# Which queue fetches the list of one pair: SyncE in one transfer in place of GpSimd in two

## The chip, the cores and the metric

The kernel runs on one core of a Trainium2 chip. The metric is device time in microseconds for one launch; less is better. Several executions of a kernel are taken, and their median is the figure that is compared. One further execution is recorded by the hardware profiler, and its trace is what the rest of this text reads.

## What is computed

A gated linear attention runs over 4 batches of 8 heads, 768 positions and 48 channels. Its output, 3072 tokens of 384 numbers, goes through a noisy top-2 router with 8 experts, each a two-layer network (384 to 1024 to 384).

```python
for t in range(S):                                   # attention
    state = alpha[:, :, t, :, None] * state + einsum('bhd,bhe->bhde', k[:, :, t], v[:, :, t])
    y[:, :, t] = einsum('bhd,bhde->bhe', q[:, :, t], state)
x = y.transpose(0, 2, 1, 3).reshape(B * S, H * D)
noisy = x @ w_gate + log1p(exp(x @ w_noise)) * noise  # router
top2 = argpartition(-noisy, 2, axis=1)[:, :2]         # with a softmax over the two as weights
for e in range(E):                                   # experts
    for k in range(2):
        mask = top2[:, k] == e
        out[mask] += top2_w[mask, k, None] * (maximum(x[mask] @ w1[e], 0) @ w2[e])
```

All numbers are float32.

## The kernel before

**Two stages that overlap.** In the first quarter of the span the attention is worked off in 24 chunks of 128 tokens. Each chunk's result is written to the DRAM tensor `x_rows`. The router runs along with it, in units of six chunks. For every token and each of its two experts it writes one entry of four numbers (token, weight, the other expert, rank) into the DRAM tensor `table`, at a row that belongs to the expert. That is done by 48 indirect transfers on GpSimd (`put_entries`, line 161), each of 128 entries of 16 bytes.

**Pairs.** The experts then take their tokens in 24 pairs of tiles, 256 list entries each. A list `order_of` (line 987) says which expert a pair belongs to: pairs 0 to 7 are the first 256 entries of experts 0 to 7, pairs 8 and 9 are two further parts of expert 7, pairs 10 and 11 of expert 6, and so on down to expert 0. A pair loads new weights only where its expert differs from that of the pair before (`is_new`, line 990), so pairs 8 and 9 use the weights that pair 7 loaded, and pair 10 is the next to load. After pair 7 there are three smaller "half" tiles in between, which start later than everything discussed here. The rows of the first 14 pairs (`PLANNED`, line 989) are known when the program is built; later ones are read from a computed plan.

**Steps of a pair.** `pair_steps(i)` (line 1184) gives each step of pair i a due time in units in which a pair takes T = 20. All steps of all pairs are sorted by due time and issued in that order; the tile framework does not reorder them (`tc.manual_schedule()`). So the due times set the order on each engine. [...] The steps that matter here, each with the due time relative to the pair's start:

- `load_tab` (-32, line 1016): fetches the pair's 256 entries from `table` into an on-chip tile `tab`. It may read any row, so it must wait for the table writes: pairs 0 to 7 for the writes of the first two of four router units, later pairs for all 48 (`take_tile`, line 169).
- `load_w1` (-29.5) and `load_w2` (-19.8): 1.5 MB of weights each, on SyncE. Each has two buffers, so a load waits until the expert two before it no longer needs the buffer.
- `find_rows` (-27; for pair 8 due at -21.5): six small VectorE operations on `tab` (lines 1046 to 1058) that give `where`, the row numbers for the gathers.
- `gather` (-26; for pair 8 -21): two indirect GpSimd transfers of 128 rows of `x_rows` into `x_in` (line 886).
- `turn_x` (-10.1, line 1064): TensorE transposes of `x_in` (line 1068).
- `product1`, `product2` (0 to 18.6, lines 1126 and 1133): TensorE products of the two layers, with VectorE sums in between (`plus`, `less`, lines 1073 to 1077). Twice per pair TensorE adds to a bank that VectorE must first have read.
- `get_prev` (8.5, line 871), `combine` (20.9, line 1158), `put_pair` (22.2, line 879): rows of `out` that already hold the token's first expert are fetched, added to and written back, by indirect transfers on GpSimd. A fetch waits for all earlier writes of `out`.

With these due times `load_tab(8)` is due at 128. On GpSimd it stands behind the last two table writes (due 125 and 126.3) and ahead of `get_prev(6)` (128.5) and `gather(8)` (139). `find_rows(8)` (138.5) stands in VectorE's queue in the midst of pair 6's last sums and pair 7's first.

**Queues.** `load_tab` puts its transfers on SyncE (SP) or on GpSimd (POOL), by pair. SP's queue otherwise holds only the weight loads in this stage. Every transfer takes one of eight completion semaphores per kind of queue in rotation, and a transfer also waits for the one eight places earlier.

Of the kernel before, what the change touches and what calls it, by code (L numbers as in the profile page):

```python
# [18 lines left out]
def kernel(  # L19
# [32 lines left out]
    nc = tc.nc  # L52
    B, H, S, D = q.shape
    N, DM = out.shape
    E, _, F = moe_w1.shape
# [113 lines left out]
    def take_tile(get, units=NU):  # L169
        count = 1 + 2 * UT // C * units  # L170
        for put in entries[:count]:
            tc.add_manual_dep(get.ins, put.name, AFTER, reason="reads any row of the table that these fill")
        for put in entries[count:]:
            tc.declare_no_dep(get.ins, put, reason="rows behind those of the tile")
        taken.append(get.ins)
# [714 lines left out]
    def of_plan(i, what, most, engine=mybir.EngineType.SP):  # L890
        return nc.values_load(plan[0:1, i, what:what + 1], engines=[engine], min_val=0, max_val=most,
                              skip_runtime_bounds_check_because=WHY)
# [101 lines left out]
    def pairs(on):  # L994
# [20 lines left out]

        def load_tab(i):

            by, engine = (nc.sync, mybir.EngineType.SP) if i < 2 or 5 <= i < E else (nc.gpsimd, mybir.EngineType.Pool)
            row = order_of[i] * RMAX + [0, R2, 2 * R2][rounds[i]] if i < PLANNED else of_plan(FIRST_PAIR + i - E, 1, TROWS - R2, engine)
            tabs[i] = on["tab"].tile([C, 2, 8], F32, name="tab")  # L1020
            parts = 1 if i < E else 2
            for s in range(parts):
                take_tile(by.dma_start(out=tabs[i][:, ds(s, 2 // parts), 0:4],
                                       in_=table.bitcast(F32)[ds(row + s * C, R2 // parts), :].rearrange("(s p) w -> p s w", p=C)),
                          2 if i < E else NU)
# [158 lines left out]
        def steps(i):  # L1184
# [5 lines left out]
            at = lambda name, t: early.get(name, T * i + t) - T * i  # L1190
            return [(T * i + t, go) for t, go in (
                (at("tab", -32.0), lambda: load_tab(i)), (at("w1", -29.5), lambda: load_w1(i)), (at("w2", -19.8), lambda: load_w2(i)),
                (at("find", -27.0), lambda: find_rows(i)), (at("gather", -26.0), lambda: gather(i)),
                (at("turn", -10.1), lambda: turn_x(i)), (at("sum_x", -7.9), lambda: sum_x(i)),
# [256 lines left out]
```

## Time and profile before

| | |
|---|---|
| median of three runs | 687.25 us (685.63 to 691.16) |
| the profiled execution's own time | 689.81 us |
| its span, first to last instruction | 688.1 us |
| mean granted TensorE clock | 0.992 of full speed |
| TensorE busy | 671.0 us, 98% |
| VectorE busy | 455.3 us, 66% |
| GpSimd busy | 319.9 us, 46% |
| DMA, queue of SP (q1) | 80.37 MB, 41.8% of 16 engines' span |
| DMA, queue of GpSimd (q0) | 23.80 MB, 11.3% |

How to read it: TensorE is at work nearly all the time, so a change shows in the time only where it adds or removes a pause of TensorE or slows its clock. Busy shares of other engines, taken over the span, do not say whether an engine was late at one place. That is read from the waits, and from the timeline around a wait: each line of a timeline has the start, the duration, the engine, the line of the kernel, the operation, written tile<-read tiles, the count, and in brackets how long the engine stood idle before it and what ended that. "SPq" lines are issues of transfers on SyncE; they are not counted as busy.

### The profile page before, as it was taken

Reading aid. Unit: us, or ns where it says so; the run is one execution under the profiler, and the core shown is the slowest. Engines: PE = TensorE matmul, PEld = TensorE weight load, DVE = VectorE, ACT = ScalarE, POOL = GpSimd, SP = SyncE. Lnnn points to the kernel's source line nnn. Section 1 sums busy time; section 2 is a strip of 40 time slices with the busy share of each in tenths; the row PEclk is TensorE's granted clock in tenths of the full one; section 3 lists DMA queues with packets and bytes.
Section 4 is the critical chain, followed back from the end, with each engine's and each line's share of the span. In section 5 each row is a group of like instructions: output and inputs, shape, how many; then the busy total and the mean of one; then the engine's idle time right before and its main releaser. Section 6 shows DMA issues by size and latency. Waiting matters only on the chain. (4 is left out here: it accounts for less than half of the span.)

```text
span 688.1 us, 15191 instructions
## 1 busy us (share of the span) xinstructions
PE 671.0 (98%) x5777; PEld 628.8 (91%) x5777; DVE 455.3 (66%) x1058; ACT 260.1 (38%) x561; POOL 319.9 (46%) x418
## 2 busy tenths in 40 slices
PE   8999999999899999998999999999999999999994
PEld 6888888888899999998999999988999889998894
DVE  8777879776678888775476667565475654756532
ACT  4455556444443324332233332324323243232430
POOL 5452386783344576774523445413455124542131
PEclk9999999999999999999899999999999999999998
DMA  9776767768756657685204476137372373720011
GB/s 185 158 173 135 155 114 142 161 131 262 279 181 226 230 158 212 187 212 195 87 10 137 140 236 230 56 114 257 120 240 61 116 249 130 235 67 26 31 55 46
DMA packets 144071, 105.65 MB, mean 154 GB/s; under 512 B 109139, under 2 KB 131359, under 8 KB 143988
## 3 DMA queue, kind: packets, MB, share of 16 engines
q1 hardware_dynamic: 131444, 80.37, 41.8%
q0 software_dynamic: 12400, 23.80, 11.3%
q8 instruction: 48, 0.79, 0.5%
q10 hardware_dynamic: 144, 0.41, 0.1%
q14 instruction: 35, 0.29, 0.1%
HBM read 95.19 MB, written 14.96 MB: 160 GB/s over the span
## 5 line engine op out<-in xcount | busy, mean ns | idle before, releaser
L886 POOL DMA_INDIRECT x_in<-x_rows,where x48 | 53.5, 1114 | 129.8 <-PE h_ps L1137 78.0
L879 POOL DMA_INDIRECT out_dram<-prev,where x48 | 52.4, 1092 | 57.2 <-DVE prev L1158 41.9
L871 POOL DMA_INDIRECT prev<-out_dram,where x48 | 54.2, 1129 | 48.8 <-issue 30.1
L1130 PE MATMUL sc<-xs,ws 128*128 128x128 f32 x576 | 73.1, 276 | 0.0
L1130 PE MATMUL sc<-xt,w 128*128 128x128 f32 x576 | 72.2, 275 | 0.0
L1137 PE MATMUL o_ps<-wt,hx 128*128 128x192 f32 x384 | 70.3, 326 | 0.0
L1141 ACT ACTIVATE h<-h 128x512 f32<-128x512 f32 x72 | 45.4, 631 | 63.9 <-DVE h L1077 63.9
L1130 PEld LDWEIGHTS sc<-xt,w 128*128 128x128 f32 x576 | 69.1, 192 | 0.0
L1130 PEld LDWEIGHTS sc<-xs,ws 128*128 128x128 f32 x576 | 68.3, 192 | 0.2 <-ACT m L1201 0.2
L1137 PEld LDWEIGHTS o_ps<-wt,hx 128*128 128x128 f32 x384 | 63.7, 190 | 0.0
L161 POOL DMA_INDIRECT table<-entry,place_u x48 | 54.4, 1133 | 16.0 <-issue 15.0
L1077 DVE TENSOR_TENSOR h<-sc,m 128x512 f32<-128x512 f32 x48 | 33.0, 690 | 41.7 <-PE sc L1130 38.5
L1130 PE MATMUL sc<-xs,w 128*128 128x128 f32 x384 | 51.0, 288 | 4.9 <-DVE h L1077 4.9
L1130 PEld LDWEIGHTS sc<-xs,w 128*128 128x128 f32 x384 | 46.3, 197 | 8.6 <-DVE h L1077 6.5
L1130 PE MATMUL h_ps<-xt,w 128*128 128x128 f32 x384 | 47.1, 276 | 0.0
L369 POOL TENSOR_TENSOR k_P<-k_P,over 128x512 f32<-128x512 f32 (+1 forms) x25 | 28.8, 1152 | 39.0 <-DVE over L353 32.0
L1146 ACT ACTIVATE o<-o_ps,tab 128x192 f32<-128x192 f32 x23 | 9.6, 419 | 95.8 <-PE o_ps L1137 95.8
L1130 PEld LDWEIGHTS h_ps<-xt,w 128*128 128x128 f32 x384 | 44.8, 192 | 0.2
L326 PE MATMUL tp<-ident,ins 128*128 128x128 f32 x288 | 43.7, 289 | 0.3 <-ACT k_P L363 0.2
L345 DVE TENSOR_TENSOR_SCAN P_all<-shared,least 128x516 f32<-128x516 f32 (+1 forms) x25 | 30.3, 1214 | 16.5 <-ACT shared L340 12.0
L1077 DVE TENSOR_TENSOR h<-h_ps,m 128x512 f32<-128x512 f32 x24 | 16.6, 690 | 35.1 <-PE h_ps L1130 35.0
L1074 DVE TENSOR_TENSOR hx<-h,hx 128x512 f32<-128x512 f32 x24 | 16.6, 693 | 33.9 <-ACT h L1141 33.8
(236 smaller groups left out, 1445.4 us busy)
## 6 DMA issues: line engine op xcount, KB each, us to landing
w<-in_moe_w_dram SPq DMA_DIRECT2D x30, 1536.0 KB, 7.6
ins<-in_alpha_dram SPq DMA_DIRECT2D x24, 192.0 KB, 3.4
ins<-in_k_dram SPq DMA_DIRECT2D x24, 192.0 KB, 4.8
ins<-in_q_dram SPq DMA_DIRECT2D x24, 192.0 KB, 4.4
vt<-in_v_dram SPq DMA_DIRECT2D x24, 192.0 KB, 3.8
x_rows<-y_sb SPq DMA_DIRECT2D x24, 192.0 KB, 5.7
ins<-in_moe_w_dram SPq DMA_DIRECT2D x3, 1536.0 KB, 12.2
shared<-in_moe_w_dram SPq DMA_DIRECT2D x3, 1536.0 KB, 6.8
```

The costliest lines, as they stand in the source:

```text
L161: put = nc.gpsimd.indirect_dma_start(out=table, out_offset=bass.IndirectOffsetOnAxis(ap=place, axis=0), in_=entry, in_offset=None, bounds_ ...
L326: nc.tensor.transpose(tp[:, j, :], src[:, 2 * j:2 * j + 2, :], ident)
L345: nc.vector.tensor_tensor_scan(P_all[:, at], a_all[:, at], least.rearrange("p j t -> p (j t)")[:, at], 0.0, op0=ALU.mult, op1=ALU.max)
L369: nc.gpsimd.tensor_tensor(c["k"][:, at], c["k"][:, at], over[:, at, 1:CB], op=ALU.mult)
L871: get = nc.gpsimd.indirect_dma_start(out=rows.bitcast(U32), out_offset=None, in_=out.bitcast(U32), in_offset=bass.IndirectOffsetOnAxis(ap= ...
L879: put = nc.gpsimd.indirect_dma_start(out=out, out_offset=bass.IndirectOffsetOnAxis(ap=at, axis=0), in_=rows, in_offset=None, bounds_check= ...
L886: nc.gpsimd.indirect_dma_start(out=rows, out_offset=None, in_=x_rows[0:units * UT, :], in_offset=bass.IndirectOffsetOnAxis(ap=at, axis=0), ...
L1074: nc.vector.tensor_tensor(to, p, q, op=ALU.subtract)
L1077: nc.vector.tensor_tensor(to, p, q, op=ALU.add)
L1130: nc.tensor.matmul(bank[name][:, f, :], W[:, ds(f * C, C)], X, start=new and f == 0, stop=True, skip_group_check=True)
L1137: nc.tensor.matmul(bank[name], H[:, f, :], W[:, f, :], start=new and f == 0, stop=True, skip_group_check=True)
L1141: nc.scalar.activation(t, t if src is None else src, AF.Relu)
```

## The change

In `load_tab`, two bounds move by one. The pair with i = 8, the first after the eight experts' first pairs, goes from the GpSimd branch to the SyncE branch, and it goes from two transfers of 128 entries to one of 256 entries (the same 4 KB into the same tile). What it waits for is not changed: the condition of `take_tile` still has `i < E`, so pair 8 waits for all 48 table writes.

```diff
         def load_tab(i):
 
-            by, engine = (nc.sync, mybir.EngineType.SP) if i < 2 or 5 <= i < E else (nc.gpsimd, mybir.EngineType.Pool)
+            by, engine = (nc.sync, mybir.EngineType.SP) if i < 2 or 5 <= i <= E else (nc.gpsimd, mybir.EngineType.Pool)
             row = order_of[i] * RMAX + [0, R2, 2 * R2][rounds[i]] if i < PLANNED else of_plan(FIRST_PAIR + i - E, 1, TROWS - R2, engine)
             tabs[i] = on["tab"].tile([C, 2, 8], F32, name="tab")
-            parts = 1 if i < E else 2
+            parts = 1 if i <= E else 2
             for s in range(parts):
                 take_tile(by.dma_start(out=tabs[i][:, ds(s, 2 // parts), 0:4],
                                        in_=table.bitcast(F32)[ds(row + s * C, R2 // parts), :].rearrange("(s p) w -> p s w", p=C)),
                           2 if i < E else NU)
```

On the engines this makes the following difference. GpSimd loses two transfers between the last table write and `get_prev(6)`. SP gains one, between the second-layer weights of pair 7 and the first-layer weights of pair 10. VectorE's and ScalarE's instructions and their order stay the same; those that use `tab` of pair 8 now wait for one semaphore of SP's kind in place of two of GpSimd's. The later transfers of both queues take other semaphores of the rotation.

## The prediction

> **What bounds the kernel now.** I read the page's busy shares and clock row first, then TensorE's waits, then the timelines of the engines around the longest one.
>
> ```profile
> PE 671.0 (98%) x5777; PEld 628.8 (91%) x5777; DVE 455.3 (66%) x1058; ACT 260.1 (38%) x561; POOL 319.9 (46%) x418
> ...
> PEclk9999999999999999999899999999999999999998
> ```
>
> TensorE (PE) is the bound. Its clock row has one weak slice inside the span, the 20th (about 327 to 344 us). The waits of TensorE hold one line of weight, 4.9 us in two waits, the longest 3.0:
>
> ```profile
> PE sc L1130 <- DVE h L1077: 4.9, 2, 3.0
> ```
>
> The timeline of TensorE, in pair 6 (first three lines) and pair 7, has that wait:
>
> ```profile
> 302.86 2.05 PE L1130 MATMUL sc<-xs,w 128*128 128x128 f32 x16
> 304.75 0.82 PE L1068 MATMUL x_ps<-ident,x_in 128*128 128x128 f32 x6
> 305.40 1.47 PE L1137 MATMUL o_ps<-w,h 128*128 128x192 f32 x8
> ...
> 321.08 1.95 PE L1130 MATMUL sc<-xt,w 128*128 128x128 f32 x16
> 326.03 3.78 PE L1130 MATMUL sc<-xs,w 128*128 128x128 f32 x16 [3.00 <-DVE h L1077]
> 329.61 1.49 PE L1068 MATMUL x_ps<-ident,x_in 128*128 128x128 f32 x6
> 330.88 2.11 PE L1137 MATMUL o_ps<-w,h 128*128 128x192 f32 x8
> ```
>
> Pair 7 stops for 3.00 us, and then the same operations take longer: 3.58 us from line to line in place of 1.89, 1.27 in place of 0.65. The stretch table shows the clock at half there (columns: stretch, length, busy of PE, PEld, DVE, ACT, POOL, clock, DMA share, GB/s):
>
> ```profile
> 326.00:328.00 2.00, 1.97 (x9) 1.97 (x10) 1.27 (x3) 1.23 (x2) 1.69 (x3) 0.50 0.40 151
> 328.00:330.00 2.00, 2.00 (x11) 2.00 (x11) 0.69 (x1) 0.00 (x0) 0.83 (x2) 0.50 0.37 105
> 330.00:332.00 2.00, 2.00 (x10) 2.00 (x9) 0.00 (x0) 1.29 (x3) 0.00 (x0) 0.50 0.01 4
> ```
>
> The timelines of VectorE, then GpSimd, say why TensorE waited:
>
> ```profile
> 312.44 0.95 DVE L1074 TENSOR_TENSOR wt<-w,wt 128x768 f32<-128x768 f32 x1
> 320.64 0.17 DVE L1046 TENSOR_SCALAR tab<-tab 128x2 f32<-128x2 f32 x1 [7.26 <-DMA tab<-table]
> ```
>
> ```profile
> 306.89 1.37 POOL L161 DMA_INDIRECT table<-entry,place_u  x1 [0.30 <-issue]
> 314.39 1.15 POOL L1023 DMA_DIRECT2D tab<-table  x2 [6.13 <-DMA table<-entry,place_u]
> ```
>
> GpSimd waits for the last table write, issues the two fetches of pair 8's list, and VectorE, which stands at `find_rows(8)` from 313.39, gets the list at 320.64. From there it needs 5.3 us to the bank read that TensorE waits for (end about 325.95). TensorE was ready at 323.03.
>
> Why both landings were slow stands in SP's timeline: weights of pair 10, 1.5 MB each, at 304.94 and 313.40. Their landing times, 8.6 and 7.5 us, end at 313.5 and 320.9. The last table write landed at 313.8, the list by 320.6: each small transfer came in as a weight load ended.
>
> [...] the pause was 3.0 us, the slow stretch about 6. [...] SP's list fetches land 11.4 us after issue (median) where they stand 0.4 us behind 1.5 MB of weights. [...] So the wait for the table moves to SP, with all that SP has queued.
>
> **The change, part by part.**
>
> *GpSimd* loses two issues of 0.574 us (the 1.15 us at 314.39) and the 6.13 us wait. Next in its queue is `get_prev(6)`, which must still wait for pair 5's output writes (issued 302.83 and 304.11, landing 5.0 to 5.4 later, so 309.1). It goes out near 309 and 310.5 in place of 315.84 and 317.21. GpSimd is not on the path; alone this is worth nothing, but the rows arrive early for `combine(6)`.
>
> *SP* gains one issue (0.574 us in the earlier SP fetches) and eight semaphore waits (17 to 43 ns each where the trace shows one that doesn't block; at most 0.35). It is free for this from 293.86, when pair 7's second weights are out. Behind the wait stand the weights of pair 10, ready at 304.94 and 313.40. They now go out after the list, near 311.5 and 313.5. They are first summed for pair 10, some 40 us later, which hides 7 us of delay: cost nothing.
>
> *The last table write* is issued at 306.89 as before, but no weights stream beside it. Table writes land in 3.5 us at best (235 to 262 us) and this one took 7.2: between 310.4 and 314.1. I take 311.
>
> *The list*: [...] The first pair's SP fetch at 155.83 had VectorE going at 157.5, 1.7 us later; GpSimd's median landing is 3.0. So VectorE gets it between 312.2 (310.4 + 0.1 + 1.7) and 317.2 (314.1 + 0.1 + 3.0); I take 313.4, just when VectorE arrives. The bank read then ends by 318.7, at the late end by 322.5; TensorE arrives at 323.03. So even the late end leaves TensorE without a wait.
>
> *What is late next*: pair 8's gather. `where` is ready at about 314.3, so it goes out at 314.7 and 316.1 in place of 322.12 and 324.03, but into 3 MB of weights streaming from 311.5 to about 327 (two times 7.5 to 8.6). TensorE wants `x_in` at 323.03 + 1.9 = 324.9. Gathers land in 3.0 to 4.9 us where the trace shows it; the slowest GpSimd row fetch beside weights, `get_prev(5)` at 288.65, took 8.9. So second half between 319.1 and 325.0: a wait of 0 to 0.1; if rows come only as the stream ends, about 2.
>
> *Sum*, against the profiled execution (689.81, span 688.1). The wait: -3.00. The slow clock: from the resumed matmuls to the next pair's first, pair 7 takes 340.64 - 326.03 = 14.61; pair 6 took 314.50 - 302.86 = 11.64; so -2.97. Together -5.97, giving 683.84. TensorE has no other wait over 1.9 us, so nothing later takes the gain back. The median of the three runs is 2.56 below the profiled one. Applied in full it gives 681.3; if those 2.56 are a smaller pause and clock drop in the median run, 683.8. I take **682.5** for the median.
>
> **The rivals.**
> 1. *The stall moves to the gather* (16%). For it: table write, list and (at 245.6, landing 5.7) row fetches came in as a weight load ended, and two loads now run back to back. Against: pair 7's gathers at 295.93 and 297.28, beside weights issued at 293.49, made no wait. A pause of 2 us, with or without a part of the clock drop, leaves a gain of 1 to 4: 683.3 to 688.8, likely 685.
> 2. *The list is slow on SP* (7%): the other side. SP's rows say 11.4 us. If the weights issued 0.4 us after it share its way, it arrives at 311.1 + 11.4 = 322.5, VectorE starts 1.9 us later than now, TensorE pauses 4.9 us in place of 3.0: 689 or, with a longer clock drop, 692. It decides from a landing of 9.5 us (320.64 - 311.1). Against: each of those fetches stood behind the weights, this one ahead.
> 3. *The change does not reach typical runs* (9%): runs of 685.63 and 691.16 differ by about as much as the stall; if the faster ones hardly have it, the median gains 1 to 3: 684.3 to 686.3.
>
> **How the numbers follow.** The likeliest case, stall and clock drop gone, has 68%, its own range 680.3 to 684.3. Over it and the rivals 1 and 3, 679.8 to 686.5 leaves out about 2 in 10. A change of 1%, about what a measurement of this kernel can tell, is 6.87 us; 5.97 is 0.87%. Over 1% faster (below 680.4) needs a median run that loses more than the profiled one: 18%. Over 1% slower (above 694.1) needs rival 2 at its worst: 4%. Within: 78%.
>
> **What would show it.** Right: no DVE wait over 3 us before L1046 near 313; SP's list issue between 310 and 314 and the two weight issues after it; TensorE's gap at 323 and the 0.50 stretch gone, pair 7 taking 20 us from start to start like pair 6. The gather step is wrong if TensorE or PEld waits before L1068 near 325 for `x_in`; the list step, if L1046 still waits to 320; the write step, if SP issues the list after 314. The prediction fails if a new pause of over 2 us stands anywhere after 313, or if the clock still falls.

## The result, and the profile after

| | before | changed |
|---|---|---|
| median of 21 runs each | 690.38 us (685.63 to 696.73) | 686.25 us (683.35 to 688.33) |
| ratio | | 0.9942, 95% interval 0.9922 to 0.9963 |
| profiled execution, its own time | 689.81 us | 687.56 us |
| its span | 688.1 us | 685.5 us |

The change makes the kernel faster by about 0.6%, some 4 us. The two profiled executions differ by only 2.25 us, and the timeline of TensorE in the changed kernel says why. Its first line is pair 0, the next two pair 6, the next four pair 7, the last the start of pair 8:

```profile
184.46 3.46 PE L1130 MATMUL sc<-xs,w 128*128 128x128 f32 x16 [3.93 <-DVE h L1077]
...
306.36 2.05 PE L1130 MATMUL sc<-xs,w 128*128 128x128 f32 x16
308.25 0.82 PE L1068 MATMUL x_ps<-ident,x_in 128*128 128x128 f32 x6
...
318.15 1.14 PE L1130 MATMUL sc<-xt,w 128*128 128x128 f32 x8
...
324.58 1.95 PE L1130 MATMUL sc<-xt,w 128*128 128x128 f32 x16
326.50 2.05 PE L1130 MATMUL sc<-xs,w 128*128 128x128 f32 x16
328.38 0.82 PE L1068 MATMUL x_ps<-ident,x_in 128*128 128x128 f32 x6
...
338.14 1.05 PE L1130 MATMUL sc<-xt,w 128*128 128x128 f32 x8
```

The starts of pair 7 and pair 8 in the kernel before:

```profile
314.64 1.14 PE L1130 MATMUL sc<-xt,w 128*128 128x128 f32 x8
...
340.64 1.05 PE L1130 MATMUL sc<-xt,w 128*128 128x128 f32 x8
```

Pair 7 now runs like pair 6: no pause, and a granted clock of 1.00 from 320 to 338 us. From its first matmul to the next pair's first it takes 338.14 - 318.15 = 19.99 us; before it took 340.64 - 314.64 = 26.00. So the change brought 6.01 us there. But pair 0, which the change doesn't touch, paused for 3.93 us in this execution, and its next 16 matmuls took 3.46 us, at a granted clock of 0.50 from 184.46 to 186 us; in the one before it paused for 1.89, and they took 2.05 at 1.00. That is 2.04 us more of pause and 1.41 more of slow clock, and everything from pair 1 on stands 3.5 us later here (306.36 against 302.86 for the same matmul of pair 6). 6.01 less 3.50 is 2.5, about the difference of the spans (2.6).

The issues of SyncE in the changed kernel, then GpSimd's instructions:

```profile
296.99 0.37 SPq L898 DMA_DIRECT2D w<-in_moe_w_dram  x1
314.52 0.37 SPq L1023 DMA_DIRECT2D tab<-table  x1
315.00 0.40 SPq L896 DMA_DIRECT2D w<-in_moe_w_dram  x1
316.90 0.37 SPq L898 DMA_DIRECT2D w<-in_moe_w_dram  x1
```

```profile
310.94 1.42 POOL L161 DMA_INDIRECT table<-entry,place_u  x1 [0.30 <-issue]
313.48 1.30 POOL L871 DMA_INDIRECT prev<-out_dram,where  x1 [1.12 <-DMA out_dram<-prev,where]
315.08 1.01 POOL L871 DMA_INDIRECT prev<-out_dram,where  x1 [0.30 <-DVE o L1149]
318.61 1.78 POOL L886 DMA_INDIRECT x_in<-x_rows,where  x1 [2.51 <-PE count L454]
```

The last table write goes out at 310.94 and SyncE, which waits for it, issues the list at 314.52, 3.6 us later; before the change GpSimd, which waited for it then, could issue the list only 7.5 us after the write (306.89 to 314.39). The first weights of pair 10 come behind the list: by the times of the kernel before, shifted by 3.5 us, they were ready at 308.4, and they go out at 315.00. The second go out at 316.90, which is their time before (313.40) shifted by the same 3.5 us; they are not held back. VectorE gets the list almost at once:

```profile
317.13 0.17 DVE L1046 TENSOR_SCALAR tab<-tab 128x2 f32<-128x2 f32 x1 [0.24 <-DMA tab<-table]
...
319.44 0.60 DVE L1158 SCALAR_TENSOR_TENSOR prev<-prev,tab,o 128x384 f32<-128x384 f32 x1
321.73 0.62 DVE L1158 SCALAR_TENSOR_TENSOR prev<-prev,tab,o 128x384 f32<-128x384 f32 x1 [1.69 <-DMA prev<-out_dram,where]
...
325.75 1.51 DVE L1077 TENSOR_TENSOR h<-sc,m 128x512 f32<-128x512 f32 x2 [1.93 <-PE sc L1130]
```

It waits 0.24 us for the list in place of 7.26. There is a new wait of 1.69 us for the second half of `get_prev(6)`, which was issued at 315.08, together with the first weights. It costs nothing: at the bank read that TensorE depends on, VectorE stands waiting for TensorE (1.93 us), not the other way round.

### The profile page after: what moved, and what is told of

Its sections match the earlier page's. It is cut to its first block, busy times and chain, and to the rows that moved or that the text cites. A ratio compares the mean times of both kernels' runs of the same rounds, so it can differ in the third digit from the quotient of the medians.

```text
span 685.5 us, 15192 instructions
## 1 busy us (share of the span) xinstructions
PE 668.8 (98%) x5777; PEld 626.8 (91%) x5777; DVE 455.9 (67%) x1058; ACT 260.1 (38%) x561; POOL 320.4 (47%) x416
```

## The experiments

Three explanations had to be told apart, since the change does three things at once: the queue (SyncE for GpSimd), the count (one transfer for two), and, since the weights of pair 10 stand behind the list in SyncE's queue, it holds the first 1.5 MB of them back until the table is written and the list is on its way. My theory was the third.

**e1: SyncE, but two transfers.** Edit to the changed kernel:

```diff
-            parts = 1 if i <= E else 2
+            parts = 1 if i < E else 2
```

> Pair 8's list on SyncE, but still in two transfers. Theory (what helps is that SyncE's wait holds back pair 10's weights): the two issues cost 2 x 0.4 to 0.6 us on an idle queue, so as the changed kernel: no wait of TensorE over 0.5 us in pair 7 and no half clock there; time within 0.3% of the changed kernel, 0.994 of before. Rival (the single transfer is what helps): the wait of TensorE in pair 7 comes back at 2 us or more.

Measured: ratio to before 0.9914 (0.9891 to 0.9936), median 684.54 us. VectorE, then TensorE in pair 7:

```profile
314.25 0.17 DVE L1046 TENSOR_SCALAR tab<-tab 128x2 f32<-128x2 f32 x1 [0.48 <-DMA tab<-table]
```

```profile
323.37 2.05 PE L1130 MATMUL sc<-xs,w 128*128 128x128 f32 x16
```

VectorE waits 0.48 us for the list, TensorE not at all. The count of transfers isn't what helped.

**e2: GpSimd, but one transfer.** The same line of the kernel before with `i <= E`.

> Pair 8's list on GpSimd as before, in one transfer in place of two. Theory (weights held back): nothing is held back, so the last table write still lands about 7 us after its issue, the list comes in as a weight load ends, VectorE waits 6 to 7 us at the list, TensorE 2 to 3 us, clock at half afterwards; ratio to before 0.998 to 1.002. Rival (the single transfer): VectorE's wait falls below 3 us and TensorE's wait is gone, ratio 0.994.

Measured: ratio 1.0001 (0.9979 to 1.0024). GpSimd, VectorE and TensorE in its timelines:

```profile
309.26 0.97 POOL L161 DMA_INDIRECT table<-entry,place_u  x1 [0.31 <-issue]
316.72 0.75 POOL L1023 DMA_DIRECT2D tab<-table  x1 [6.48 <-issue]
```

```profile
322.65 0.17 DVE L1046 TENSOR_SCALAR tab<-tab 128x2 f32<-128x2 f32 x1 [6.71 <-DMA tab<-table]
```

```profile
328.04 2.46 PE L1130 MATMUL sc<-xs,w 128*128 128x128 f32 x16 [2.46 <-DVE h L1077]
330.30 1.49 PE L1068 MATMUL x_ps<-ident,x_in 128*128 128x128 f32 x6
```

All three waits are close to those of the kernel before (6.13, 7.26 and 3.00 us), and the transposes take 1.49 us in place of 0.82: the granted clock was 0.50 again, from 330 to 332 us. One transfer in place of two on the old queue is worth nothing.

**e3: GpSimd's fetch as before, SyncE only holds the weights.** Edit to the kernel before; the extra tile is read by nothing:

```diff
             parts = 1 if i < E else 2
+            if i == E:
+                gate = one.tile([C, 2, 4], F32, name="gate")
+                take_tile(nc.sync.dma_start(out=gate, in_=table.bitcast(F32)[ds(row, R2), :].rearrange("(s p) w -> p s w", p=C)))
             for s in range(parts):
```

> The list of pair 8 is fetched by GpSimd in two transfers as before; in addition SyncE fetches the same rows into a tile that nothing reads, at the place where the changed kernel fetches the list, so that pair 10's weights stand behind the same wait. Theory (weights held back): the last table write lands within 4.5 us of its issue in place of about 7, the list fetch goes out with it, and VectorE's wait falls to 0 to 4 us; TensorE's wait in pair 7 is 0 to 0.5 us, ratio 0.993 to 0.996. Rival (GpSimd's queue is what is slow): the list still comes 5 us or more after its issue, TensorE waits 2 us or more, ratio 0.998 to 1.002.

Measured: ratio 0.9934 (0.9896 to 0.9972), median of 10 runs 684.66 us, so a gain like that of the change, with the list still on GpSimd in two transfers. Its lines from the added ones on lie three further down than in the kernel before. SyncE, GpSimd, then VectorE:

```profile
310.51 0.37 SPq L1024 DMA_DIRECT2D gate<-table  x1
310.99 1.53 SPq L896 DMA_DIRECT2D w<-in_moe_w_dram  x1
313.51 0.37 SPq L898 DMA_DIRECT2D w<-in_moe_w_dram  x1
```

```profile
307.01 1.37 POOL L161 DMA_INDIRECT table<-entry,place_u  x1 [0.30 <-issue]
311.04 1.15 POOL L1026 DMA_DIRECT2D tab<-table  x2 [2.66 <-ACT n L1149]
```

```profile
313.66 0.17 DVE L1049 TENSOR_SCALAR tab<-tab 128x2 f32<-128x2 f32 x1 [0.16 <-DMA tab<-table]
```

The same two fetches go out 4.0 us after the last table write's issue in place of 7.5, and VectorE waits 0.16 us in place of 7.26. (The bracket of the GpSimd line names ScalarE; by the program the wait is for the table writes.) What has gone is the weight traffic in this stretch. The last two columns of these lines are the DMA share and GB/s, from the last table write's issue to the list's, and from there to VectorE's start; the kernel before, then e3:

```profile
306.89:314.39 7.50, 7.50 (x48) 7.50 (x48) 5.91 (x13) 1.26 (x3) 1.37 (x2) 1.00 0.57 204
314.39:320.64 6.25, 6.25 (x57) 6.22 (x56) 0.00 (x0) 2.17 (x4) 3.23 (x4) 1.00 0.98 303
```

```profile
307.01:311.04 4.03, 4.03 (x26) 4.03 (x26) 4.00 (x10) 1.26 (x3) 1.37 (x1) 1.00 0.05 5
311.04:313.66 2.62, 2.62 (x19) 2.62 (x18) 1.91 (x4) 0.00 (x0) 2.22 (x3) 1.00 0.31 36
```

This is the run that decides: on GpSimd's queue as before, the two stretches took 4.03 and 2.62 us in place of 7.50 and 6.25 once the weights were out of the way.

**e4: first weights ahead of the list, second behind.** Edit to the changed kernel's table of early due times:

```diff
-            early = {0: EARLY_0, 1: EARLY_1, E: {"find": T * E - 21.5, "gather": T * E - 21.0}}.get(i, {})
+            early = {0: EARLY_0, 1: EARLY_1, E: {"tab": T * E - 30.5, "find": T * E - 21.5, "gather": T * E - 21.0}, E + 2: {"w1": T * E - 30.6}}.get(i, {})
```

> As the changed kernel, but pair 10's first-layer weights are issued ahead of the list on SyncE, as early as before the change; only the second-layer weights stand behind the wait. Theory: the last table write shares the engines with the first weights again and lands about 7 us after its issue; the list follows in 2 to 3 us, so VectorE gets it 9.5 to 10.5 us after the last table write's issue, against 13.75 before and the 10.8 from which TensorE waits: VectorE's wait 3 to 5 us, TensorE's 0 to 0.5; ratio 0.993 to 0.997. If holding back the first weights is what counts, TensorE waits over 1 us and the ratio is 0.997 or more.

Measured: ratio 0.9943 (0.9920 to 0.9966), median 685.80 us. SyncE, then VectorE:

```profile
308.59 0.37 SPq L896 DMA_DIRECT2D w<-in_moe_w_dram  x1
318.75 0.37 SPq L1023 DMA_DIRECT2D tab<-table  x1
319.28 0.37 SPq L898 DMA_DIRECT2D w<-in_moe_w_dram  x1
```

```profile
321.14 0.17 DVE L1046 TENSOR_SCALAR tab<-tab 128x2 f32<-128x2 f32 x1 [4.10 <-DMA tab<-table]
```

The last table write was issued at 311.09, 2.5 us after the first weights. The list could go out only at 318.75, 7.7 us later, as slow as before. But ahead of the second weights the list itself took 2.4 us, and it came 10.05 us after the write's issue. In the kernel before it came 13.75 us after (306.89 to 320.64) and TensorE waited 3.00, so TensorE waits from about 10.8; here it had no pause in pair 7. So keeping the list alone clear of a weight load is enough for TensorE, with under 1 us to spare; with the table write clear too, it comes 6.2 us after (changed kernel) to 7.0 (e1), some 4 us before TensorE would wait. The table write alone was not tried.

**e5 to e9: the pause in pair 0.** The changed kernel's 21 runs fall into two groups, 683.35 to 685.55 us at a mean TensorE clock of 0.995 to 0.997 and 686.25 to 688.33 at 0.992 or 0.993, and its profile, one of the second group, has the 3.93 us pause in pair 0. VectorE's timeline of the changed kernel names the reason:

```profile
180.46 0.69 DVE L1077 TENSOR_TENSOR ws<-w 128x512 f32<-128x512 f32 x1 [5.46 <-DMA w<-in_moe_w_dram]
```

VectorE stands at the first sum of pair 1's weights until they land, with the bank reads of pair 0 behind it. The edit, in the due times of pair 1, puts the two sums behind those reads:

```diff
-        EARLY_1 = {"tab": -301.0, "find": -0.5, "gather": -0.4, "w1": 0.5, "w2": 5.0}
+        EARLY_1 = {"tab": -301.0, "find": -0.5, "gather": -0.4, "w1": 0.5, "w2": 5.0, "s0": 10.2, "s1": 10.3}
```

It was made in the changed kernel and in the kernel before.

> The changed kernel with one thing moved: VectorE's first two sums of pair 1's first-layer weights (0.69 us each) are due at 10.2 and 10.3 of pair 0 in place of 3.5 and 4.2, behind the two bank reads that TensorE waits for. Theory (the time still lost, and the spread of the runs over 683 to 688 us, is the pause of TensorE in pair 0, where VectorE stands 3 to 5 us at these sums until the weights land): the pause in pair 0, 1.9 to 3.9 us with up to 1.4 us of slow clock, falls below 0.5 us; the median is 680 to 683 us and the spread below 3 us. Rival (the early pause is paid back by other waits, or the spread is noise of the chip): median 685 to 687, spread as before.

> The kernel before with the same two sums of pair 1 moved, so that the pause of pair 0 is out of both. The difference to the changed kernel with the sums moved is what the changed list fetch is worth by itself. Theory (pair 7's pause with its slow clock is there in every run, 6 us): 5 to 6.5 us slower than the changed kernel with the sums moved, so 686 to 689 us, and its spread stays at several us. Rival (typical runs have a smaller pause in pair 7 than the profiled one): only 2 to 4.5 us slower.

These two decide nothing about the change: both medians of 6 runs were 714.38 us, on a chip on which the kernel before took 716.94. Pair 7's pause is not there in e6, although it has the old fetch:

```profile
326.28 2.08 PE L1130 MATMUL sc<-xt,ws 128*128 128x128 f32 x8 [5.32 <-ACT m L1206]
...
352.18 2.05 PE L1130 MATMUL sc<-xs,w 128*128 128x128 f32 x16
```

TensorE stopped for 3.09 and 5.32 us in pair 6, so that pair 7 came later against the list: VectorE found it there (no wait at L1046), and the matmuls of the last line, those that waited for 3.00 us in the kernel before, have no wait. Pair 0 has no pause in e5 and e6. Why TensorE stopped in pair 6 on this chip is open; where the list isn't late, the change has nothing to gain. Both were run again on another chip, with the changed kernel beside them.

> The changed kernel with VectorE's first two sums of pair 1's first-layer weights due at 10.2 and 10.3 of pair 0 in place of 3.5 and 4.2, a second time, since the first runs of it were on a chip on which every kernel took some 27 us longer. Theory (what is left of the early pause and its slow clock is in pair 0, at these sums): 1.5 to 4 us faster than the changed kernel of the same call, spread below 3 us, no wait of TensorE over 0.6 us in pair 0. Rival (the early pause is paid back later): within 0.7 us of the changed kernel.

> The kernel before with the same two sums moved, a second time. Theory (pair 7's pause with its slow clock is there in every run, 6 us): 5 to 6.5 us slower than the changed kernel with the sums moved. Rival (typical runs have a smaller pause in pair 7 than the profiled one): 2 to 4.5 us slower. The profile shows TensorE's wait of 2 to 3 us in pair 7 and none in pair 0.

> The changed kernel again, beside the two with the sums moved. Both theories: 0.994 of before, runs in two groups some 3.5 us apart, by whether TensorE's clock fell after the pause in pair 0; no wait of TensorE in pair 7.

| | runs | median | range | ratio to before (690.10 us here) |
|---|---|---|---|---|
| e9, changed kernel | 22 | 685.21 us | 682.61 to 689.64 | 0.9933 (0.9910 to 0.9956) |
| e7, changed, sums moved | 8 | 683.30 us | 682.61 to 684.76 | 0.9895 (0.9859 to 0.9931) |
| e8, before, sums moved | 22 | 688.98 us | 685.75 to 692.41 | 0.9973 (0.9951 to 0.9994) |

In e9 the runs lie in two groups again (682.61 to 685.38 and 686.55 to 689.64), and pair 7 has no pause. TensorE's waits in e7 (engine, line, what it waited for; us in total, times, longest), the three longest:

```profile
PE y L1360 <- POOL ones L99: 1.3, 1, 1.3
PE sc L390 <- DVE q_P L379: 0.5, 1, 0.5
PE o_ps L417 <- ACT k_end L404: 0.4, 1, 0.4
```

No pause of the expert stage is left among them, the median is lower by 1.9 us than the changed kernel's, and the spread is 2.2 us in place of 7.0. So most of the spread of the changed kernel was the pause in pair 0. (Fewer runs alone would not narrow it so: 8 of e9's runs, drawn at random, span 6 us in the median. The interval of e7's ratio overlaps with e9's; the spread and the profile carry this, more than the medians.) In e8 pair 0 is clean and pair 7 has its pause:

```profile
326.49 3.16 PE L1130 MATMUL sc<-xs,w 128*128 128x128 f32 x16 [3.23 <-DVE h L1077]
329.44 1.40 PE L1068 MATMUL x_ps<-ident,x_in 128*128 128x128 f32 x6
```

With pair 0 out of both, the change is worth 688.98 - 683.30 = 5.68 us. That lies in the 5 to 6.5 of the theory; typical runs do have the pause in pair 7. What it costs varies: e8's runs still spread over 6.7 us.

e7 has the lowest median of the versions that were run.

## Why the prediction was right, and where a size was off

*The bound, the pause and the slow clock.* As written: the pause and the slow clock are gone, and pair 7 became shorter by 6.01 us against the 5.97 of the sum. That the two would go together was my estimate, from one profile in which the clock of 0.50 follows the pause of 3.00 us.

*The last table write.* I took 4.1 us from issue to landing; the list, which waits for it, went out 3.6 us after its issue. e3 shows the reason given for it, the missing weight stream, alone and without a change of queue; with the first weights back, in e4, the write was as slow as before.

*The list on SyncE.* Taken at 1.7 to 3.0 us; 2.4 us from its issue to VectorE's start in e4, 2.6 in the changed kernel. Rival 2, the 11.4 us of the earlier fetches, didn't happen. Those of pairs 5 to 7 stood 0.4 us behind 1.5 MB of weights in the same queue (issued at 233.54, 253.64 and 273.55 in the kernel before), this one 0.5 us ahead of such a load.

*What is late next.* The gather of pair 8 went out into the weight stream (318.61 and 320.70) and cost nothing: the transposes of `x_in` at 328.38 follow the matmuls without a wait. Rival 1 didn't happen. What did come late was `get_prev(6)`, by 1.69 us, which I had called early; less the 3.5 us by which this execution is late, it went out 1 us after the time I gave, and met the weights.

*Weights of pair 10.* The first were held back by 6.6 us (308.4 to 315.00), the second not at all, at no cost, as written: they are first summed at 362.05.

*The median.* This is the term that was mis-sized. I gave 682.5 us; 686.25 was measured, 0.25 us inside the upper end of the range, and the gain was about 4.1 us (0.37% to 0.78%), not 6. Two things are in it. First the level: I went below the sum's 683.84 because three runs had a median of 687.25, under the profiled execution. 21 runs gave 690.38, 0.6 above the profiled 689.81, so the profiled execution was the typical one; the whole 5.97 off 690.38 gives 684.4. Second, the other 1.9 us: I read from one execution that TensorE's second wait, "over 1.9 us", is a constant that is in both kernels. It isn't: pair 0's pause was between 0.96 us (e3) and 3.93 (changed kernel) in seven profiles with the old order of the sums, with and without slow clock. It adds a few us of chance to each run; that it accounts for the 1.9 us of the medians isn't shown. That the measured median still fell into the range is in part luck. The likeliest case came true in its mechanism, but its own range, 680.3 to 684.3, was missed; the upper end of 686.5 stood there for rivals 1 and 3.

Rival 3 (typical runs lack the pause in pair 7) was wrong: e8 against e7 gives 5.68 us by the medians. With pair 0's pause in place the medians gain 4.1 and 4.9 us in the changed kernel (first runs and e9), 6.1, 6.0 and 4.9 in e1, e3 and e4, and 5.7 without it. Why they differ isn't settled; by their intervals they need not.

## What to carry to other kernels

In this kernel a wait on SyncE's queue also held what stood behind it (weights, for 6.6 us after they could have gone out), and that was the useful part: from the last table write's issue to the list's it took 3.58 us in place of 7.50, and from there to VectorE's start 2.6 in place of 6.25, because 1.5 MB of weights, first used 47 us after their issue, had to queue behind them. When a small transfer on the path lands just as a bulk transfer ends, look at what else is being moved in that stretch (here the DMA share was 0.57 and 0.98, and 0.05 and 0.31 in e3) before changing its queue or its size, and test it with a gate that only delays the bulk. And an operation that may wait for a transfer does not belong in front of the reads that the bounding engine depends on, if it isn't needed soon: moving two sums of 0.69 us took the pause of 1.0 to 3.9 us out of pair 0, and the spread went from 7.0 to 2.2 us.

## What the runs showed of the hardware

- Small transfers beside a bulk load took 1.9 to 2.5 times as long. The last table write (128 entries of 16 bytes) held its successor up for 7.5 to 7.7 us from its issue where 1.5 MB of weights had been issued 1.8 to 2.5 us before it (before, e2, e4, e8), and for 3.2 to 4.0 where they were held back (changed, e1, e3, e7, e9). The 4 KB list in two GpSimd transfers took 6.25 us from issue to VectorE's start beside the weights (before) and 2.62 ahead of their data (e3); in one transfer 5.9 us beside them (e2, GpSimd) and 2.4 ahead of them (e4, SyncE).
- The length of the pause alone doesn't tell whether TensorE's clock falls in these runs. The 16 matmuls that took 2.05 us at a granted clock of 1.00 (before, pairs 0 and 6) took 2.05 after pauses of 0.96, 1.53, 1.89 and 2.31 us (pair 0 in e3, e9, before, e1), but 3.58 after 1.97 (e2, pair 0), 3.78 after 3.00 (before, pair 7, clock 0.50), 2.46 after 2.46 with slow transposes behind them (e2, pair 7, clock 0.88 from 328 to 330 us and 0.50 from 330 to 332), 3.16 after 3.23 (e8, pair 7), 3.05 after 3.84 (e4, pair 0) and 3.46 after 3.93 (changed, pair 0, clock 0.50). So a pause of 1.97 us had a slow stretch behind it and one of 2.31 us had none; what decides is open.
